# Storing most of an attention-and-MoE output as fp16 tiles cast by the software DMA queue instead of fp32 tiles on the sync queue

## The chip, the cores and the metric

The kernel runs on one core of a Trainium2 chip. The metric is the device time of one execution in microseconds (us). Times are medians of several executions. The span of a profiled execution, which the trace covers, is about 2 us shorter than the time. "Software queue" is the DMA queue that GpSimd (POOL) feeds, "sync queue" the one that SyncE (SP) feeds. The profile counts the packets of both queues against the same 16 DMA engines of the core.

## The reference

Sliding-window attention, plain in half of the heads and dilated in the other half, is followed by a soft mixture of experts. Only the last line of it matters here: each of 4608 rows is a weighted sum of 32 expert slots, and the result is 4608 x 512 in fp32, 9.44 MB.

```python
def _moe_ref(x, phi, w1, w2):
    logits = x @ phi                                    # 4608 x 32
    # ... slot inputs, one two-layer MLP for each of 8 experts -> slot_out (32 x 512)
    c = logits - logits.max(1, keepdims=True)
    c = np.exp(c)
    c /= c.sum(1, keepdims=True) + 1e-09
    return (c @ slot_out).astype(np.float32)            # 4608 x 512
```

## The kernel before

The attention and the experts' first layer take until about 140 us and aren't touched. While they run, GpSimd loads the experts' weights with a cast from fp32 to fp16. At the end these loads are what the kernel waits for. So `slot_out` is computed in two halves of 256 columns: the left half of `w2` of the last two experts is loaded first, and the left half of the output for the first 8 row pairs (a pair is 256 rows) is computed and stored while the right half of the weights still comes in. Then follow 10 pairs of whole rows, and last the right halves of the first 8 pairs.

```python
out_pool = tc.alloc_tile_pool(name="outp", bufs=NSPLIT // 2)          # 8 buffers for "ot"

def combine(half, pair):                                              # 256 rows x 256 columns
    # ... two matmuls into a PSUM tile fp [128, 2, 256]
    ot = out_pool.tile([128, 2, NH], FP32, name=f"ot{half}_{pair}", tag="ot")
    # even pair: two ScalarE activations; odd pair: one VectorE multiply; both: ot = fp * rrow
    nc.sync.dma_start(out=out[r0 : r0 + 256, NH * half : NH * half + NH]..., in_=ot)

def combine_full(pair):                                               # 256 rows x 512 columns
    ot = out_pool.tile([128, 2, DMODEL], FP32, name=f"of_{pair}", tag="of", bufs=5)
    # ... one matmul, and one eviction for each 128 rows: k = 0 on ScalarE, k = 1 on VectorE
    nc.sync.dma_start(out=out[r0 : r0 + 256, :]..., in_=ot)

# slot_out(half, experts): matmuls into PSUM; after the last expert ScalarE copies the half to so_sb
slot_out(0, ORDER[:6]); slot_out(1, ORDER[:6]); slot_out(0, HALVED)
for pair in range(8):                    # left halves; one expert of slot_out(1) after pair 5
    combine(0, pair)
    # ...
slot_out(1, HALVED[1:])
for pair in range(8, 18):
    combine_full(pair)
for pair in range(8):
    combine(1, pair)                     # right halves
```

The softmax here doesn't subtract the row's maximum and nothing guards it: scores larger than these inputs give would overflow.

## Time and profile before

| what | value | where it is read |
|---|---|---|
| time | 184.87 us (184.70 to 185.29, 4 runs) | times |
| span of the profiled run | 182.8 us | page |
| last weight load landed | 156.95 us | chain |
| stores under way | 155 to 181.3 us | windows, DMA packets |
| rate of whole-row stores (2 KB packets) | 384 GB/s | windows, 161 to 170 us |
| rate of half-row stores (1 KB packets) | 342 to 344 GB/s | windows, 175 to 180 us |
| eviction of 128x512 | ScalarE 0.69 us, VectorE 0.75 us | tile view |

First the page of the kernel before: the busy share of the DMA engines (tenths, in 40 slices of the span), the rate in each slice, and the two DMA queues with packets, MB and share of the 16 engines' span.

```profile
DMA  5999999999999999999999999999999999999996
GB/s 88 195 198 211 203 208 206 211 209 204 213 207 204 213 208 204 213 208 204 213 208 204 212 212 213 216 214 214 215 214 216 196 196 183 328 376 387 380 351 219
...
q0 software_dynamic: 24640, 31.10, 97.6%
q1 hardware_dynamic: 7360, 9.56, 14.9%
```

The DMA engines are full in all slices but the first and the last. The first 33 slices show about 210 GB/s because loads are counted by their fp16 side: the page has 62.18 MB read from HBM for 31.10 MB in q0, so fp32 comes out of HBM at twice that rate. The last slices are the fp32 stores of the sync queue (q1), counted in full.

Now the windows view of the kernel before: start and end, length, then busy us of PE, PEld, DVE, ACT and POOL with the count of instructions, the granted PE clock, the DMA busy share and GB/s. The DMA share is the summed time of the packets over 16 engines; above 1.0, packets on one engine overlap in time.

```profile
161.00:163.00 2.00, 1.18 (x5) 0.29 (x3) 0.80 (x2) 0.16 (x1) 0.00 (x0) 1.00 1.05 385
...
165.00:170.00 5.00, 3.07 (x11) 1.22 (x10) 3.27 (x5) 3.10 (x6) 0.00 (x0) 0.66 1.04 384
...
175.00:178.00 3.00, 0.00 (x0) 0.00 (x0) 0.00 (x0) 0.00 (x0) 0.00 (x0) 0.50 1.03 344
178.00:180.00 2.00, 0.00 (x0) 0.00 (x0) 0.00 (x0) 0.00 (x0) 0.00 (x0) 0.50 1.03 342
```

In these stretches, and in those left out between 159 and 180 us, the DMA share never falls under 1.0, while VectorE and ScalarE are each busy for two thirds of a stretch at most between 161 and 175 us, and idle after that. Nothing but the stores sets the pace here.

The chain of waits of the kernel before (start, length, what) tells the same.

```profile
146.53 10.42 DMA w<-in_moe_w_dram
...
157.33 0.38 ACT so_sb L689
...
158.17 3.00 ACT of L732 x5
...
162.03 10.45 DMA out_dram<-of x2
```

The last load lands at 156.95 us, ScalarE copies the right half of `so_sb`, evictions start, and then the stores fill the rest. Two lines of ScalarE's timeline (start, busy us, what, idle time before it and what ended it) show when that happens: the evictions of left pair 6, and the copy.

```profile
155.90 0.84 ACT L709 ACTIVATE ot<-f,rrow 128x256 f32<-128x256 f32 x2 [0.67 <-PE f L697]
157.33 0.37 ACT L689 CAST so_sb<-so 128x256 f16<-128x256 f32 x1 [0.59 <-PE so L681]
```

Line 792 is the end of the program; the columns are count, shortest/median/longest in ns, and first to last start in us.

```profile
L792 POOLq EVENT_SEMAPHORE  x4: 17/17/17, 182.1 to 182.7; - x4
L792 POOLq DRAIN  x3: 51/98/11675, 146.5 to 182.5; - x3
L792 SPq DRAIN  x3: 7/7/7, 182.0 to 182.3; - x3
```

SP starts its end routine (its first DRAIN) at 182.0 us, when all stores have landed. POOL's long DRAIN began at 146.5 us, together with GpSimd's last load issue, and took 11.7 us, so it was over at 158.2 us and nobody noticed. POOL's first semaphore of the final barrier comes at 182.1 us, right behind SP.

### The profile page before, as it was taken

How to read it: one execution, taken by the hardware profiler on the slowest of the kernel's cores; microseconds unless marked ns; L12 is line 12 of the kernel's file. 1: busy time of each engine (PE TensorE's matmuls, PEld its weight loads, DVE VectorE, ACT ScalarE, POOL GpSimd, SP SyncE). 2: the span in 40 equal slices, each digit the busy share in tenths (PEclk: the TensorE clock that was granted, in tenths of full speed). 3: DMA queues.
4: the chain of work that ended last, by engine and by line, in shares of the span. 5: the costliest groups of instructions: out<-in, count | busy, mean ns of one | idle time of the engine just before them, and what ended most of it. 6: DMA issues, size and time to landing. Idle time of an engine off the chain costs nothing.

```text
span 182.8 us, 5535 instructions
## 1 busy us (share of the span) xinstructions
PE 142.9 (78%) x2448; PEld 85.6 (47%) x2448; DVE 104.2 (57%) x225; ACT 90.1 (49%) x161; POOL 62.6 (34%) x86
## 2 busy tenths in 40 slices
PE   0467989999999999999999999998694087746600
PEld 0134556557557557557557557573532063312300
DVE  2585797958767867867867865360502004555700
ACT  2044267667666766766766766734002005644800
POOL 7643644652651751751822935311110110000000
PEclk9999999999999999999999999985569667897555
DMA  5999999999999999999999999999999999999996
GB/s 88 195 198 211 203 208 206 211 209 204 213 207 204 213 208 204 213 208 204 213 208 204 212 212 213 216 214 214 215 214 216 196 196 183 328 376 387 380 351 219
DMA packets 32024, 41.01 MB, mean 224 GB/s; under 512 B 2144, under 2 KB 19680, under 8 KB 32000
## 3 DMA queue, kind: packets, MB, share of 16 engines
q0 software_dynamic: 24640, 31.10, 97.6%
q1 hardware_dynamic: 7360, 9.56, 14.9%
q8 instruction: 19, 0.31, 0.6%
q14 instruction: 5, 0.04, 0.1%
HBM read 62.18 MB, written 9.44 MB: 392 GB/s over the span
## 4 chain that ended last, share of the span: by engine, by line
DMA 48%; PE 27%; issue 7%; ACT 6%; POOL 4%; DVE 3%; SPq 0%; POOLq 0%
DMA w<-in_moe_w_dram 34%; DMA raw<-in_q_dram 8%; DMA out_dram<-of 6%; PE lg L413 5%; PE o_p L344 5%; PE sa L287 4%; ACT p L298 4%; PE sa L276 3%; PE sb L276 3%; ACT of L732 2%; PE u L455 2%; PE rd L394 1%; PE vb L188 1%; PE va L188 1%; POOL w L220 1%
## 5 line engine op out<-in xcount | busy, mean ns | idle before, releaser
L298 ACT ACTIVATE p<-sa 128x960 f16<-128x960 f32 (+2 forms) x24 | 21.4, 890 | 30.2 <-PE sb L287 29.5
L344 PEld LDWEIGHTS <-p 128*128 128x128 f16 (+2 forms) x544 | 19.5, 98 | 12.6 <-issue 8.6
L241 DVE STREAM_TRANSPOSE qk<-raw 128x576 uint32<-128x576 uint32 x16 | 20.0, 1250 | 6.8 <-DMA raw<-in_q_dram 5.9
L250 DVE STREAM_TRANSPOSE qk<-raw 128x320 uint32<-128x320 uint32 (+1 forms) x32 | 21.5, 678 | 0.3
L298 ACT ACTIVATE p<-sb 128x960 f16<-128x960 f32 (+2 forms) x24 | 21.2, 885 | 0.0
L276 PE MATMUL sa<-masks,ident 128*128 128x480 f16 (+2 forms) x48 | 13.8, 372 | 6.6 <-DMA ident<-ident_d 4.9
L413 PE MATMUL lg<-xTd,phi 128*128 128x288 f16 x32 | 18.3, 659 | 0.0
L287 PE MATMUL sa<-qk 32*128 32x160 f16 (+4 forms) x416 | 15.7, 212 | 2.4 <-DVE qk L241 2.4
L287 PEld LDWEIGHTS <-qk 32*128 32x128 f16 x832 | 11.9, 96 | 11.8 <-issue 8.2
L276 PEld LDWEIGHTS <-ident 128*128 128x128 f16 x96 | 8.9, 102 | 17.4 <-issue 8.7
L216 POOL COPY v<-v 32x1024 f16<-32x1024 f16 x8 | 8.3, 1034 | 25.4 <-DVE v L209 22.9
L344 PE MATMUL o_p<-v,p 128*128 128x65 f16 (+1 forms) x288 | 16.4, 201 | 0.7 <-ACT v L197 0.7
L287 PE MATMUL sb<-qk 32*128 32x160 f16 (+4 forms) x416 | 15.7, 212 | 0.0
L232 POOL DMA_DIRECT2D w<-in_moe_w_dram x8 | 5.9, 742 | 27.2 <-DMA w<-in_moe_w_dram 22.8
L366 DVE TENSOR_TENSOR xp<-o_p,rc_p 128x448 f16<-128x448 f32 (+1 forms) x24 | 14.5, 602 | 0.8
L366 DVE TENSOR_TENSOR xd<-o_d,rc_d 128x448 f16<-128x448 f32 (+1 forms) x24 | 14.5, 602 | 0.8
L713 DVE TENSOR_TENSOR ot<-f,rrow 128x512 f32<-128x512 f32 x8 | 5.5, 690 | 15.8 <-PE f L697 15.6
L276 PE MATMUL sb<-masks,ident 128*128 128x480 f16 (+2 forms) x48 | 14.0, 372 | 0.4 <-issue 0.2
L681 PE MATMUL so<-w,hTm 128*32 128x256 f16 x128 | 7.0, 354 | 8.5 <-DMA w<-in_moe_w_dram 7.7
L220 POOL DMA_DIRECT2D w<-in_moe_w_dram x16 | 11.4, 715 | 5.5 <-DMA raw<-in_k_dram 2.1
L188 PE MATMUL va<-vs,orders 32*128 32x256 f16 (+1 forms) x96 | 12.1, 289 | 1.0 <-ACT p L298 1.0
L417 ACT ACTIVATE ET<-lg 128x288 f16<-128x288 f32 x16 | 6.6, 410 | 12.0 <-PE lg L413 11.8
(84 smaller groups left out, 251.7 us busy)
## 6 DMA issues: line engine op xcount, KB each, us to landing
w<-in_moe_w_dram POOLq DMA_DIRECT2D x16, 512.0 KB, 16.6
w<-in_moe_w_dram POOLq DMA_DIRECT2D x6, 1024.0 KB, 28.1
out_dram<-of SPq DMA_DIRECT2D x10, 512.0 KB, 5.5
vs<-in_v_dram POOLq DMA_DIRECT2D x8, 512.0 KB, 13.1
out_dram<-ot SPq DMA_DIRECT2D x16, 256.0 KB, 3.9
raw<-in_q_dram POOLq DMA_DIRECT2D x7, 576.0 KB, 15.1
raw<-in_k_dram POOLq DMA_DIRECT2D x7, 576.0 KB, 15.4
w<-in_moe_w_dram POOLq DMA_DIRECT2D x8, 256.0 KB, 23.3
```

Of the source, the lines that this page charges most:

```text
L188: nc.tensor.matmul(o.rearrange("p (h d) -> p h d", h=4), l, st[:, 0:4, D * r : D * r + D], start=(r == 0), stop=(r == DIL - 1), skip_group ...
L216: nc.gpsimd.tensor_copy(out=vL[b % NV][0:32, :, :, 0:D], in_=vD[b % NV][96:128, :, :, 0:D])
L220: nc.gpsimd.dma_start(out=w1t[e][:, 2 * i : 2 * i + 2, :], in_=src[:, 2 * i : 2 * i + 2, :])
L241: nc.vector.transpose(out=dst, in_=src)
L250: nc.vector.transpose(out=o, in_=i)
L276: nc.tensor.matmul(sps[h // 2][:, h % 2, 0:n], ident, bias[g], start=True, stop=False, skip_group_check=True,)
L287: nc.tensor.matmul(sps[h // 2][:, h % 2, c0 : c0 + w], kt_[32 * h : 32 * h + 32, k0 : k0 + 128, tt], qt_[32 * h : 32 * h + 32, q0 : q0 + w ...
L298: nc.scalar.activation(out=pt, in_=sps[ab][:, :, 0:n], func=AF.Exp, scale=SCALE)
L344: nc.tensor.matmul(o[p0 : p0 + np_, n, :], l, rr, start=(k == 0), stop=(k == len(jobs) - 1), skip_group_check=True,)
L366: nc.vector.tensor_tensor(out=x.rearrange("p t (h d) -> p (t h) d", h=4)[0:nq, u0:u1, :], in0=o[0:nq, 0:n, 0:D], in1=rc[0:nq, 0:n, None].b ...
L413: nc.tensor.matmul(lp, phi4[:, kc].rearrange("p c s -> p (c s)"), rhs, start=(kc == 0), stop=(kc == 3))
L681: nc.tensor.matmul(so[half][32 * a : 32 * a + 32, :], hTm[2 * g + c // 4][:, c % 4, 32 * j : 32 * j + 32], w2t[e][:, c, NH * half : NH * h ...
```

## The change

The intent: half of the bytes are read from SBUF for most stores, output tiles are half as big, so that there can be more of them, and the right halves don't wait for the end. A casting DMA has to be issued by GpSimd: the Trainium skill, "DMA: Bandwidth & Descriptors", section "SWDGE vs HWDGE vs iDMA", lists a cast during DMA as possible on the software queue only. The left halves stay on the sync queue in fp32, since they run beside the last loads.

```diff
-    out_pool = tc.alloc_tile_pool(name="outp", bufs=NSPLIT // 2)
+    out_pool = tc.alloc_tile_pool(name="outp", bufs=1)
 ...
     def combine(half, pair):
-        ot = out_pool.tile([128, 2, NH], FP32, name=f"ot{half}_{pair}", tag="ot")
+        ot = out_pool.tile([128, 2, NH], (FP32, FP16)[half], name=f"ot{half}_{pair}", tag=f"ot{half}", bufs=6 + 2 * half)
 ...
-        nc.sync.dma_start(
+        (nc.sync, nc.gpsimd)[half].dma_start(
 ...
     def combine_full(pair):
-        ot = out_pool.tile([128, 2, DMODEL], FP32, name=f"of_{pair}", tag="of", bufs=5)
+        ot = out_pool.tile([128, 2, DMODEL], FP16, name=f"of_{pair}", tag="of", bufs=7)
 ...
-        nc.sync.dma_start(
+        nc.gpsimd.dma_start(
 ...
         for pair in range(NSPLIT // 2, NFIN // 2):
             combine_full(pair)
-        for pair in range(NSPLIT // 2):
-            combine(1, pair)
+            if pair >= NFIN // 2 - NSPLIT // 2:
+                combine(1, pair - (NFIN // 2 - NSPLIT // 2))
```

## The prediction

> **What bounds the kernel now.** The chain of waits ends with weight loads (the last lands at 156.95 us), one PE and ACT step each, five ACT evictions, and then 10.45 us of stores. From 155 us on the windows show the DMA engines at a busy share of 1.03 to 1.05 until 181 us, while PE, ACT and DVE are half idle. So the last 25 us are DMA time: 9.44 MB of output. While 2 KB packets (whole rows) are stored the windows show 383 to 386 GB/s, while 1 KB packets (halves) are stored 343 to 357.
>
> **What the change does not remove.** HBM still gets 9.44 MB of fp32. PE, ACT and DVE do the same instructions in another order. Evictions from PSUM (ACT 128x512 0.69 us, DVE 0.75 us) should keep their times. The Trainium skill, "DMA: Bandwidth & Descriptors", section "Issuing engines are not separate DMA queues", says that DMAs of all issuers share the same 16 engines and only issue time is saved. SP's issue time (0.66 us per half, 1.22 us per 512 KB) is hidden under the stores (1.37 us per 512 KB at 384 GB/s) already.
>
> **What it may gain.** The SBUF side of 18 stores (7.34 MB) is read as fp16. If the write side limits a store, nothing is gained. The casting loads of this trace run at 2 x 213 = 426 GB/s on their fp32 side (2 KB fp16 packets) and at 2 x 198 = 396 with 512 B fp16 packets. If casting stores reached those rates, whole rows would take 12.3 us in place of 13.7, right halves 5.3 in place of 6.0: at most 2 us. I expect about a third of it. More buffers (7 for 5) buy nothing where DMA is the limit.
>
> **What it costs.** Left halves have 6 buffers, not 8. Pair 6 on ACT now waits for pair 0's store. That was issued at 153.74 and takes 4.0 us to land, so ACT gets on at about 157.6 in place of 155.9. The second so_sb copy stands behind it on ACT and moves from 157.33 to about 158.5, the first whole row with it. Its store is issued at about 160.3 instead of 159.2, now by GpSimd (0.7 us issue, by the loads' issues). Left stores kept the engines busy until about 161, so some 0.5 to 1 us of DMA idleness appears between 159 and 162. The first left eviction and store lose their waits on eight load semaphores: 0.2 us gained.
>
> **Sum.** Delay +0.8, casting stores -0.7, start -0.2: 184.8 us, within 2%. Range 182.0 to 187.3. Faster by over 2%: 0.12. Within 2%: 0.78. Slower by over 2%: 0.10.
>
> **What would show the steps right.** (1) The span from 162 us to the end is full of DMA, with 384 to 400 GB/s of fp32 written (or half of it, if packets are counted by their fp16 side, as for the loads). (2) ACT waits for an output DMA before the pair-6 eviction, and so_sb's second copy starts 1 to 1.5 us later. (3) GpSimd issues take 0.6 to 0.9 us and aren't in the chain. (4) ACT and DVE end several us earlier, and the end is still a store landing.
>
> **What would make it wrong.** The cast may have its own rate: above 420 GB/s written gives 183 or less; 330 gives 187. If the engines' cost follows the fp16 side, stores could nearly halve and the kernel gains 5 us or more. The software queue may start later or fall behind. The left stores' landing, which shares the engines with the last loads, may be later than 4 us and stretch the gap.

## The result, and the profile after

The changed kernel takes 186.02 us (185.76 to 186.38, 4 runs) against 184.87 us: ratio 1.006, 95% interval 1.0036 to 1.0085. That is 1.1 us slower, small but clear of noise. Ratios in this document are the mean time of one kernel's runs over the mean of the other's runs of the same rounds, so they aren't quite the ratios of the medians quoted. The result is correct in fp16, too.

The rates and queues of the page after:

```profile
GB/s 88 199 204 212 202 206 208 210 207 206 214 209 203 212 210 203 213 206 206 213 207 208 209 211 216 214 215 214 214 214 212 197 196 191 319 325 405 408 410 91
...
q0 software_dynamic: 29536, 38.44, 112.6%
q1 hardware_dynamic: 2464, 2.22, 3.7%
```

38.44 MB now go through the software queue (q0) and 2.22 MB through the sync queue. The last slices reach 405 to 410 GB/s, where before they had 376 to 387 and then 351; and the last slice has only 91. The windows after show both, and a hole:

```profile
161.00:163.00 2.00, 1.99 (x8) 0.93 (x7) 1.59 (x3) 1.67 (x5) 1.42 (x2) 0.65 0.61 198
163.00:165.00 2.00, 1.55 (x6) 0.57 (x6) 1.96 (x4) 1.90 (x5) 1.96 (x3) 1.00 1.48 420
165.00:170.00 5.00, 3.91 (x18) 1.62 (x17) 4.56 (x7) 4.69 (x10) 5.00 (x8) 1.00 1.60 408
...
175.00:178.00 3.00, 0.00 (x0) 0.00 (x0) 0.00 (x0) 0.00 (x0) 0.03 (x1) 0.50 1.58 410
178.00:180.00 2.00, 0.00 (x0) 0.00 (x0) 0.00 (x0) 0.00 (x0) 0.00 (x0) 0.50 1.64 406
```

Two differences stand out against the same windows before. From 163 us on the stores run at 406 to 420 GB/s instead of 342 to 384. Between 161 and 163 us the DMA share falls to 0.61 (before: 1.05); a finer cut has 0.13 from 161.6 to 162.6 us, so the engines are idle for about one microsecond. ScalarE's timeline shows where that comes from:

```profile
157.84 0.84 ACT L709 ACTIVATE ot<-f,rrow 128x256 f32<-128x256 f32 x2 [2.09 <-DMA out_dram<-ot]
158.57 0.37 ACT L689 CAST so_sb<-so 128x256 f16<-128x256 f32 x1
```

ScalarE waited 2.09 us for an output DMA before the eviction of left pair 6 (its buffer is that of pair 0, which had to land first), and the copy of `so_sb` stands behind it in order: it starts at 158.57 instead of 157.33 us. VectorE waits likewise for pair 7. The first whole-row store is issued at 161.36 us instead of 159.20.

The end of the chain view after, and line 792 after:

```profile
173.83 0.47 issue
174.30 0.73 POOLq L792
```

```profile
L792 POOLq EVENT_SEMAPHORE  x4: 17/17/17, 183.4 to 184.0; - x4
L792 POOLq DRAIN  x3: 51/98/9061, 174.3 to 183.9; - x3
L792 SPq DRAIN  x3: 7/7/7, 181.8 to 183.6; - x3
```

The chain view is no help with the end: it is followed back from the last instruction that isn't the sequencer's, here GpSimd's last store issue, and stops at 175.03 us (before: at 173.15, with an eviction). Line 792 is where to look. SP's first DRAIN is at 181.8 us, so the stores were all in a little earlier than before (182.0). But POOL's long DRAIN, begun at 174.30 us, took 9.06 us and ended at 183.36 us. POOL's first semaphore of the final barrier comes at 183.4 us, 1.6 us behind SP. The span ends at 184.1 us. That wait is new.

The trace records when each store landed. With that, the difference of the two spans can be taken apart without a remainder (us):

| stretch | before | after | difference |
|---|---|---|---|
| up to the last left half's landing | 162.44 | 162.89 | +0.45 |
| from there to the last landing | 19.22 | 18.50 | -0.72 |
| from the last landing to the end of the span | 1.16 | 2.76 | +1.60 |
| span | 182.82 | 184.15 | +1.33 |

The first row is within the scatter of the runs: in the thirteen profiles the first left store is issued between 153.06 and 154.35 us, by kernels that hardly differ up to there. The second row holds a gain and the hole of 1 us. The third row is the drain.

### The profile page after: what moved, and what is told of

Same layout as the page of the kernel before. It is cut to its first block, busy times and chain, and to the rows that moved or that the text cites. A ratio compares the mean times of both kernels' runs of the same rounds, so it can differ in the third digit from the quotient of the medians. Undisturbed runs are those within 1.5% of the kernel's fastest.

```text
span 184.1 us, 5522 instructions
## 1 busy us (share of the span) xinstructions
PE 142.3 (77%) x2448; PEld 85.5 (46%) x2448; DVE 104.8 (57%) x225; ACT 90.0 (49%) x161; POOL 75.1 (41%) x104
## 3 DMA queue, kind: packets, MB, share of 16 engines
q0 software_dynamic: 29536, 38.44, 112.6%
q1 hardware_dynamic: 2464, 2.22, 3.7%
## 4 chain that ended last, share of the span: by engine, by line
DMA 42%; PE 30%; ACT 8%; issue 6%; POOL 6%; DVE 3%; POOLq 0%; DVEq 0%; ACTq 0%
DMA w<-in_moe_w_dram 27%; DMA vs<-in_v_dram 7%; DMA raw<-in_q_dram 6%; PE lg L413 5%; PE o_p L344 4%; PE sa L287 4%; ACT p L298 4%; PE sa L276 3%; PE sb L276 3%; ACT ot L709 3%; DMA out_dram<-ot 2%; PE f L730 2%; PE u L455 1%; PE rd L394 1%; PE vb L188 1%
## 5 line engine op out<-in xcount | busy, mean ns | idle before, releaser
L713 DVE TENSOR_TENSOR ot<-f,rrow 128x512 f32<-128x512 f32 (+1 forms) x8 | 5.5, 688 | 18.6 <-PE f L697 15.5
L743 POOL DMA_DIRECT2D out_dram<-of x10 | 7.0, 701 | 15.1 <-ACT of L732 14.0
```

## The experiments

Theory: three effects add up. (1) The cast makes the stores faster. (2) Six left buffers delay the whole rows and leave a DMA hole. (3) GpSimd's end-of-program drain outlasts the last landing of the software queue, which costs nothing as long as the sync queue ends last, and 1.6 us where the software queue ends last. Rivals: for (1), the software queue as such or the new order; for (2), GpSimd's later issue; for (3), a long backlog of the software queue, or its being used for outputs at all. Eleven kernels ran, all with correct results; the kernel before had medians of 184.73, 184.60 and 184.59 us.

### Eight left buffers in the changed kernel

```diff
-tag=f"ot{half}", bufs=6 + 2 * half)
+tag=f"ot{half}", bufs=8 - half)
```

(The space allows 8 + 7, not 8 + 8.)

> The changed kernel with 8 left buffers (and 7 right ones) instead of 6 (and 8). Theory (six left buffers stall ACT at pair 6 and open two DMA gaps, 0.4 us at 158 and 1.1 us at 162): the wait of ACT for an output DMA before pair 6 is gone, the second so_sb copy is back at 157.3 to 157.7, the DMA share stays at 0.9 or more from 157 to 162 us except for at most 0.5 us, and the span is 1.0 to 1.5 us shorter than the changed kernel's 184.1: 182.6 to 183.1. Rival (the gap comes from GpSimd's late first issue and the software queue's start, not from the buffers): the gap at 162 stays, the span gains less than 0.5 us.

Measured: 185.17 us, ratio 1.0028 (1.0015 to 1.0041). ScalarE's timeline has the copy back in its old place, and the windows have no hole:

```profile
157.24 0.37 ACT L689 CAST so_sb<-so 128x256 f16<-128x256 f32 x1 [0.61 <-PE so L681]
```

```profile
161.00:163.00 2.00, 1.45 (x8) 0.67 (x7) 1.96 (x4) 1.89 (x5) 2.00 (x4) 1.00 1.36 394
...
165.00:170.00 5.00, 2.04 (x10) 0.76 (x8) 3.21 (x5) 2.41 (x5) 4.37 (x7) 0.98 1.67 409
...
178.00:180.00 2.00, 0.00 (x0) 0.00 (x0) 0.00 (x0) 0.00 (x0) 0.00 (x0) 0.50 1.07 244
```

The hole at 161 to 163 us is gone (share 1.36). From 165 to 170 us the stores still run at 409 GB/s, and by 180 us the data are done: the last landing is at 180.31 us, against 181.66 before. Still the span is 183.2 us, longer than before. Line 792 of this run shows why:

```profile
L792 POOLq EVENT_SEMAPHORE  x4: 17/17/17, 182.3 to 183.1; - x4
L792 SPq DRAIN  x3: 7/7/7, 180.7 to 182.5; - x3
```

SP is ready at 180.7 us, POOL at 182.3. The buffers cost 0.3% (1.006 less 1.0028), 0.6 us, but the two ratios come from different calls and their intervals overlap slightly, so the size is rough; I had expected 1.0 to 1.5 from the profile, which gave 0.97. The rival for (2) falls: GpSimd's issue at 159.61 us came early enough to leave no hole.

### The software queue without the cast

```diff
 # the kernel before
-        nc.sync.dma_start(                      # in combine
+        (nc.sync, nc.gpsimd)[half].dma_start(
-        nc.sync.dma_start(                      # in combine_full
+        nc.gpsimd.dma_start(
```

> The kernel before, with whole rows and right halves issued by GpSimd on the software queue but still fp32 (no cast), order and buffers as before. Theory A (the faster stores of the changed kernel, 408 GB/s against 384 and 348, come from the halved SBUF read of the cast): rates stay at 380 to 386 GB/s for whole rows and 343 to 357 for halves, DMA share near 1.0, span 184 to 185 (end delayed by the GpSimd drain). Theory B (the software queue itself keeps more packets under way): 404 GB/s or more with a DMA share of 1.4 or more in both, span 182.5 to 183.5. Either way, theory of the end (GpSimd's last drain outlasts the last software landing by about 1.6 us): 3.0 us or more from the last DMA bytes to the end of the span, against 1.7 before.

Measured: 187.85 us, ratio 1.0174 (1.0154 to 1.0193). Its windows:

```profile
161.00:163.00 2.00, 0.52 (x2) 0.10 (x1) 0.14 (x1) 0.00 (x0) 1.62 (x3) 1.00 1.02 370
...
165.00:170.00 5.00, 2.95 (x10) 1.24 (x10) 3.09 (x5) 2.90 (x6) 2.68 (x4) 0.60 1.01 370
...
175.00:178.00 3.00, 0.00 (x0) 0.00 (x0) 0.00 (x0) 0.00 (x0) 1.64 (x3) 0.71 1.01 326
```

Whole rows at 370 GB/s, halves at 326, with a share of 1.0: not faster but slower than from the sync queue (384 and 344). So the software queue as such isn't the reason for the gain; it comes with the cast. One caution: the form of the packets changes with it. From 165 to 170 us this kernel's software queue moved 1.85 MB in 512 packets (4 KB each, apart from some of 4 bytes), one after the other (share 1.01); the changed kernel's moved 2.04 MB in 1331 (2 KB and 1 KB by the fp32 side), and they overlap (share 1.60). A casting packet of 2 KB takes longer than a plain one of the sync queue, 114 ns against 88 in the mean; the higher rate goes with the overlap. Whether fewer bytes read from SBUF or the form of the packets brings it, no run separates. The absence of a bandwidth gain fits the Trainium skill, "DMA: Bandwidth & Descriptors", section "Issuing engines are not separate DMA queues", by which another issuer saves only the time to issue; here some bandwidth was even lost. The span ends 2.76 us after the last landing, as in the changed kernel, with fp32 tiles: the drain has nothing to do with the cast. Neither theory had the lower rates, and the span, 185.6 us, lies above both ranges.

### The order alone

```diff
 # the kernel before
             combine_full(pair)
-        for pair in range(NSPLIT // 2):
-            combine(1, pair)
+            if pair >= NFIN // 2 - NSPLIT // 2:
+                combine(1, pair - (NFIN // 2 - NSPLIT // 2))
```

> The kernel before, with only the order changed: right halves between whole rows, still fp32 on the sync queue. Theory (the order by itself brings nothing, the cast brings the rate): same time as before, ratio 0.997 to 1.003, last sync landing 1.1 to 1.3 us before the end of the span, DMA at 360 to 385 GB/s with a share near 1.0. Rival (mixing 1 KB and 2 KB packets is what made the stores of the changed kernel faster): 395 GB/s or more from 164 us on and a span of 182 or less.

Measured: 184.48 us, ratio 0.9988 (0.9972 to 1.0004). Its windows have 366 to 369 GB/s from 165 to 178 us, which lies between the 384 of whole rows and the 344 of halves. So the order by itself does nothing to the time that shows.

### Six left buffers alone

```diff
 # the kernel before
-    out_pool = tc.alloc_tile_pool(name="outp", bufs=NSPLIT // 2)
+    out_pool = tc.alloc_tile_pool(name="outp", bufs=6)
```

> The kernel before, with only 6 buffers for the half-width tiles instead of 8. Theory (six left buffers hold ACT at pair 6 until pair 0 has landed, and that delays the second so_sb copy and the first whole row): ACT idles 1.5 to 2.2 us for an output DMA before pair 6, the second so_sb copy starts at 158.2 to 158.8, the first whole-row store is issued at 160.2 to 160.8, a DMA dip of 0.3 to 1 us follows near 161, and the time is 0.3 to 1.0 us over the kernel before. Rival (the dip needs the software queue's late start): ACT waits, but the time is within 0.3 us of before.

Measured: 185.53 us, ratio 1.0044 (1.0029 to 1.0059), so 0.8 us. ScalarE's timeline and the window of the hole:

```profile
158.73 0.84 ACT L709 ACTIVATE ot<-f,rrow 128x256 f32<-128x256 f32 x2 [2.87 <-DMA out_dram<-ot]
159.46 0.37 ACT L689 CAST so_sb<-so 128x256 f16<-128x256 f32 x1
```

```profile
161.00:163.00 2.00, 2.00 (x7) 0.73 (x6) 1.79 (x3) 1.63 (x4) 0.00 (x0) 0.59 0.74 260
```

The wait, 2.87 us, and with it the delay of the copy (159.46 us) were larger in this profile than I had said, since pair 0 landed only at 158.63 us (the profiled execution, 186.40 us, was the slowest of the seven); the time is within the range. The same mechanism therefore works with the sync queue alone: (2) is the buffers' doing. One caution: the right halves have 6 buffers here, too, and some of their evictions waited as well, though the sync queue was issuing without a pause by then.

### Whole rows by the software queue, right halves by the sync queue

```diff
 # the kernel before
-        ot = out_pool.tile([128, 2, DMODEL], FP32, name=f"of_{pair}", tag="of", bufs=5)
+        ot = out_pool.tile([128, 2, DMODEL], FP16, name=f"of_{pair}", tag="of", bufs=10)
-        nc.sync.dma_start(                      # in combine_full
+        nc.gpsimd.dma_start(
```

> The kernel before, with only the whole rows as fp16 on the software queue (10 buffers); left and right halves in fp32 on the sync queue, right halves last as before. Theory (drain hidden when the sync queue ends last; whole rows faster by the cast): the software queue ends 2 us or more before the sync queue, the GpSimd drain ends before the last sync landing, 1.7 us or less from the last bytes to the end, whole rows alone at 405 to 416 GB/s, span 181.0 to 182.2, faster than the kernel before by 0.5 to 1.8 us. Rival (the tail belongs to the kernel's end whenever GpSimd issued any output): 3 us or more from last bytes to the end, span not below 183.

Measured: 184.18 us, ratio 0.9973 (0.9960 to 0.9987): faster than before by 0.3%.

```profile
L792 POOLq DRAIN  x3: 51/98/13548, 165.9 to 182.4; - x3
L792 SPq DRAIN  x3: 7/7/7, 181.8 to 182.2; - x3
```

The software queue's last store landed at 177.84 us, POOL's drain was over at 179.49 us, the sync queue's last landed at 181.40 us, and the span ended 1.28 us later. So the drain is hidden, and the rival that any output from GpSimd costs a tail falls. The span, 182.7 us, missed the expected range: whole rows did run at 413 GB/s, but while both queues were active, the rate was 373 to 384.

### Right halves by the software queue, whole rows by the sync queue

```diff
 # the kernel before
-        ot = out_pool.tile([128, 2, NH], FP32, name=f"ot{half}_{pair}", tag="ot")
+        ot = out_pool.tile([128, 2, NH], (FP32, FP16)[half], name=f"ot{half}_{pair}", tag="ot")
-        nc.sync.dma_start(                      # in combine
+        (nc.sync, nc.gpsimd)[half].dma_start(
```

> The kernel before, with only the right halves as fp16 on the software queue, the whole rows in fp32 on the sync queue. Whole rows run at 384 GB/s until the right halves join at about 170 us; then both queues share. If the software queue ends last or within 1 us of the sync queue, the theory of the end wants the span to end 1.4 to 1.7 us after the last software landing: span 182.5 to 184. If mixed queues run at the faster rate, the last bytes are moved 0.5 to 1.0 us earlier than before.

Measured: 185.85 us, ratio 1.006 (1.0044 to 1.0076). The last landing (181.31 us, on the software queue) is 0.35 us earlier than before, with halves at 395 GB/s instead of 344; POOL's drain ended 1.56 us after it, and the span 2.35 us after it (I had expected 1.4 to 1.7 for the span, which fits the drain alone). The kernel is 1.7 us slower than the one above, where the queues are exchanged; 1.07 us of it is the longer end (2.35 against 1.28), with the software queue last. The rest isn't taken apart: the two kernels also differ in how many bytes are cast and in buffers.

### The last pairs of whole rows by the sync queue

Both kernels are the changed kernel with 8 left buffers. All fp16 stores come first; then the last four pairs, or the last one, are evicted as fp32 blocks of 128 rows and stored by the sync queue.

```diff
 # the changed kernel; LAST = 4, and LAST = 1
-        for pair in range(NSPLIT // 2, NFIN // 2):
-            combine_full(pair)
-            # ... right halves between them
+        first, stop = NSPLIT // 2, NFIN // 2 - LAST
+        for pair in range(first, stop):
+            combine_full(pair)                       # fp16, software queue
+            if pair >= first + 2:
+                combine(1, pair - first - 2)         # fp16, software queue
+        for pair in range(stop - first - 2, NSPLIT // 2):
+            combine(1, pair)
+        for pair in range(stop, NFIN // 2):
+            combine_rows(pair)                       # two [128, 512] fp32 tiles, sync queue
```

> Candidate for the best: the changed kernel with 8 left buffers, and the last four pairs of whole rows (2.1 MB) in fp32 on the sync queue, after all fp16 stores. Theory of the end: the software queue's last landing is 2 us or more before the sync queue's, the GpSimd drain ends (1.6 to 2.0 us after the last software landing) before the sync queue is done, and the span ends 1.1 to 1.3 us after the last sync landing. With 408 GB/s for the casting part: span 180.9 to 181.9, time 182.8 to 183.7, ratio 0.989 to 0.995. Rival (mixing the two queues costs as much as the cast gains): ratio 0.996 to 1.000.

> The same, with only the last pair of whole rows (0.5 MB) in fp32 on the sync queue. Theory of the end: 0.5 MB is not enough to outlast the software queue by 1.6 us, so the drain is still exposed: the span ends 2.6 to 2.9 us after the last software landing, span 182.3 to 183.3, slower than the kernel with four pairs by 0.7 to 1.8 us. Rival (it is the last output's queue that decides, whatever lies in the other one): span as with four pairs.

Measured: with four pairs 186.07 us (ratio 1.0074, 1.0061 to 1.0087), with one 185.22 us (ratio 1.0034, 1.0016 to 1.0051). I had the first one wrong, and the order of the two as well. With four pairs the software queue did not end first: its last landing was at 181.79 us, the sync queue's at 181.62. The two queues of that run between 175 and 177 us (packets, MB, share) show how that came about:

```profile
q1 hardware_dynamic: 262, 0.49, 90.4%
q0 software_dynamic: 264, 0.26, 47.9%
```

They got the same number of packets, 262 and 264, but those of the sync queue are 2 KB and those of the software queue, right halves by then, 1 KB. The Trainium skill, "DMA: Bandwidth & Descriptors", section "Queues, rings and completion order", says that each engine goes round-robin between queues by whole packets, each of which typically holds several descriptors. Equal counts agree with taking turns; whether a "packet" of this profile is one of the page's, no run shows. So the software queue fell behind and ended last, and the span ended 2.6 us after its last landing, as the theory of the end has it for that case. With one pair, the sync queue was done at 178.05 us and the software queue at 181.32; the span ended 2.7 us later, as expected, though at 184.0 us it lies above the expected range. Neither hides the drain; so they don't contradict the theory, but the plan for the first one was bad.

### One late store on the software queue, and its control

In the kernel before, the last store (256 KB) is made to come late: its buffer is that of right half 3, so it can be evicted only when that one has landed. The first kernel stores it as fp16 by GpSimd, the control as fp32 by SP.

```diff
 # the kernel before; the control has sw = False
+        sw = half == 1 and pair == 7
+        late = half == 1 and pair in (3, 7)
-        ot = out_pool.tile([128, 2, NH], FP32, name=f"ot{half}_{pair}", tag="ot")
+        ot = out_pool.tile([128, 2, NH], FP16 if sw else FP32, name=f"ot{half}_{pair}",
+                           tag="late" if late else "ot", bufs=1 if late else 7)
-        nc.sync.dma_start(                      # in combine
+        (nc.gpsimd if sw else nc.sync).dma_start(
```

> The kernel before, with the single last store (right half of pair 7, 256 KB of 9.44 MB) as fp16 on the software queue; its buffer is the one of right half 3, so that its eviction, and so its issue, comes after that one's landing and it lands last. Theory of the end (GpSimd's final drain lasts 1.6 to 2.0 us past the last software landing, and the span ends 0.7 to 0.8 us after it): the span ends 2.6 to 2.9 us after the last landing, and the kernel is slower than its control with the same store in fp32 on the sync queue by 1.2 to 1.8 us. Rival (the tail comes from the long backlog of the software queue): one short store leaves a tail of 1.1 to 1.6 us and the two kernels are within 0.4 us of each other.

> The control: the same buffers and the same late last eviction, but that store in fp32 on the sync queue. Both theories: the span ends 1.1 to 1.3 us after the last landing, and GpSimd's drain ends at 158 to 159 us. Time 0 to 1 us above the kernel before for the delayed last store.

Measured: 186.55 us (ratio 1.0096, 1.0075 to 1.0118) against the control's 185.13 us (ratio 1.0012, 0.9984 to 1.0040), 1.4 us for the queue of one store that holds 1/36 of the bytes. The end of the program with the software store, then that of the control:

```profile
L797 POOLq EVENT_SEMAPHORE  x4: 17/17/17, 183.7 to 184.3; - x4
L797 POOLq DRAIN  x3: 51/98/3853, 179.8 to 184.2; - x3
L797 SPq DRAIN  x3: 7/7/7, 182.7 to 183.9; - x3
```

```profile
L797 POOLq EVENT_SEMAPHORE  x4: 17/17/17, 182.7 to 183.3; - x4
L797 POOLq DRAIN  x3: 51/97/11667, 146.7 to 183.2; - x3
L797 SPq DRAIN  x3: 7/7/7, 182.6 to 182.9; - x3
```

In the first, POOL's drain began at 179.8 us and took 3.85 us. It ended at 183.65 us, 1.28 us after the store's landing at 182.37; SP had been ready at 182.7. The span ended 2.06 us after the landing, less than the 2.6 to 2.9 that I had expected. In the control the drain ended at 158 us, SP and POOL are ready together, and the span ends 1.16 us after the last landing. So 0.9 us of the 1.4 come from the end. The store's own path is longer, too: from the landing of right half 3 to that of the last store it was 3.93 us by GpSimd and 3.06 us by SP. The two shares add up to more than 1.4, as each comes from one profile. The rival "only a long backlog makes a tail" falls. So does the milder form, that a backlog makes it longer. The time from the software queue's last landing to the end of POOL's drain, in all thirteen traces by the number of stores that GpSimd issues (each kernel has the same 66 loads besides):

| software stores | 0 | 1 | 8 | 10 | 14 | 16 | 17 | 18 |
|---|---|---|---|---|---|---|---|---|
| drain ends after the last landing, us | 1.24 | 1.28 | 1.56 | 1.64 | 1.81 | 1.89 | 1.93 | 1.97 |

That is 1.24 us and 0.041 us more for each store. DMAs still under way when the drain begins don't set it: there are 8 in the kernel before, which has the shortest tail, and 6 to 8 in all others but this one. Nor do bytes, packets or the cast: all three kernels with 18 stores, the one without a cast among them, have 1.97. Fewer and larger software stores should then shorten it a little; no run tried that.

### A version that beats both

The lesson of the experiments put together: 8 left buffers; fp16 and the software queue for all right halves and eight pairs of whole rows; the last two pairs in fp32 by the sync queue, held back until the software queue is nearly done, so that the queues don't mix for long. The hold is a buffer: these tiles take the buffers of whole pair 14 and right half 6.

```diff
 # the changed kernel; combine_rows as above, its first two tiles with tags "g1" and "g2", bufs=1
+        tag, bufs = (("ot0", 8), ("g2", 1) if pair == 6 else ("ot1", 5))[half]    # in combine
+        tag, bufs = ("g1", 1) if pair == 14 else ("of", 6)                        # in combine_full
+        after_row = {10: (0,), 11: (1,), 12: (2,), 13: (3, 4, 5), 14: (6,), 15: (7,)}
+        for pair in range(NSPLIT // 2, 16):
+            combine_full(pair)
+            for p in after_row.get(pair, ()):
+                combine(1, p)
+        combine_rows(16)
+        combine_rows(17)
```

> Candidate for the best: 8 left buffers; eight whole pairs and all right halves as fp16 on the software queue; the last two whole pairs (1.05 MB) in fp32 on the sync queue, held back until whole pair 14 and right half 6 have landed (they use those buffers), so that the queues mix little and the sync queue ends last. Theory: 405 GB/s or more up to about 176 us, the sync queue's last landing 2 us or more after the software queue's last, the drain hidden, the span ends 1.1 to 1.3 us after the last landing: span 181.2 to 182.2, ratio 0.991 to 0.997. If the gate opens too late, a DMA gap shows before the sync stores; if too early, the software queue ends within 1.9 us of the sync queue and the span ends 2.6 us or more after its last landing: ratio 0.998 to 1.003.

Measured: 183.65 us, ratio 0.9947 (0.9925 to 0.9970): 0.9 us under the kernel before and about 2 us under the changed one (1.1% by the ratios). It was run at another time. Its windows and its end:

```profile
170.00:175.00 5.00, 0.00 (x0) 0.00 (x0) 0.00 (x0) 0.00 (x0) 1.64 (x3) 0.64 1.73 405
175.00:178.00 3.00, 0.00 (x0) 0.00 (x0) 1.41 (x2) 1.27 (x2) 0.00 (x0) 0.50 1.36 376
```

```profile
L812 POOLq EVENT_SEMAPHORE  x4: 17/17/17, 181.0 to 181.7; - x4
L812 POOLq DRAIN  x3: 51/98/8513, 171.2 to 181.5; - x3
L812 SPq DRAIN  x3: 7/7/7, 181.0 to 181.3; - x3
```

The casting stores run at 405 GB/s until 175 us, and the hole at 161 us isn't there (share 1.32 from 161 to 163 us). POOL's drain ends at 179.67 us (171.16 plus 8.51), 1.9 us after the software queue's last landing at 177.78; the sync queue's last landing is at 180.75 us, SP and POOL are ready together at 181.0, and the span ends at 181.8. From 175 to 178 us, where the software queue runs out and the sync queue sets in, the rate is 376 GB/s.

## Why the prediction was right or wrong

The total, 184.8 us with a range of 182.0 to 187.3, held 186.02; "within 2%" was right. That says little for the sum that led to it: it was 1.2 us too low and had no change where the kernel became 1.1 us slower. It lacked a term of 1.6 us, and part of that was made up by luck, as the faster stores gave 0.55 us more than it had. The range was wide enough for the missing term even without that.

- **What bounds the kernel.** Right: the stores' DMA time from 155 us on. What moved the time in the experiments was the stores' rate, a hole in the stores, or what follows the last one.
- **"Delay +0.8".** Right in mechanism, and in size within what two rough measures tell. ScalarE got on at 157.84 us (predicted 157.6), the copy moved to 158.57 (158.5). GpSimd's first issue came at 161.36, a microsecond later than the 160.3 predicted: VectorE had waited for its buffer as well, and GpSimd began the issue 0.57 us after the second eviction's end, SP before only 0.06 us. The hole was about 1 us (0.5 to 1). Undoing it gained 0.6 us; doing it alone cost 0.8 us.
- **"Casting stores -0.7".** Right in direction, too small. I allowed "at most 2 us" and took a third. From the last left landing to the last landing it is 19.22 us before and 17.96 us with 8 left buffers: -1.26 us. The windows from 165 us on show 406 to 410 GB/s, above the 384 to 400 of step (1) and within the 396 to 426 that the loads had suggested.
- **"Start -0.2".** Not seen. The first left store came 0.39 us later, not earlier, in the profile after; the thirteen profiles scatter by 1.3 us there, so 0.2 us couldn't show.
- **The missing term.** The sum had no term for the end of the program: step (4) said that "the end is still a store landing". It isn't: it is GpSimd's drain, and from the last landing to the end of the span it is 2.76 us instead of 1.16, +1.60 us. The profile before had the sign of it: POOL's drain ended at 158.18 us, 1.24 us after the last load. I had not looked at it, and it was off the critical path until the change made GpSimd the last to issue. Step (3) had the issue times right (0.70 to 0.72 us) and looked no further than the issues: GpSimd held up the end by its drain.
- **The sum as measured.** +0.6 for the buffers, -1.26 for the faster stores, +1.6 for the drain: about +0.9 us (an estimate that mixes times and one profile's intervals), against 1.1 us measured.

What stays open: why a casting store is faster. Half as many bytes are read from SBUF, and that is what the change set out to use, but no run tells that apart from some other property of a casting DMA, such as its packets, which overlap. And what POOL's drain does after the last landing, and why each software store adds 0.041 us to it, no trace shows.

## What to carry to other kernels

Before the last stores are moved to another queue, look at the end of the program, too: which engine's drain is then the last, and is it hidden behind another queue's stores? A casting store is worth trying where stores bound the kernel, but let the sync queue have the last stores (here 1.05 MB), held back until the software queue is nearly empty. And count buffers along each engine's order: an eviction that waits for a buffer also holds up whatever stands behind it on the same engine, here a copy on which everything else depended.

## What the Trainium skill lacked or had wrong

- "DMA: Bandwidth & Descriptors" has no rate for stores that cast. Here fp16 to fp32 stores ran at 405 to 410 GB/s, counted by their fp32 side, against 384 (2 KB packets) and 344 (1 KB) for plain stores from the sync queue.
- The same page's section "Issuing engines are not separate DMA queues" speaks of no cost of another issuer, and where the page calls the sync and scalar queues generally faster ("Issuing engine by pattern") it gives no store rates. Here the same fp32 stores were slower from GpSimd: 370 against 384 GB/s for whole rows, 326 against 344 for halves, and the kernel 1.7% slower, 1.6 us of it at the end.
- No page that I read tells that GpSimd's drain at the end of the program outlasts its last DMA. "VectorE: DVE Perf Modes", section "The DRAIN you can't avoid", speaks of drains of the preamble and postamble of about 12 ns on all five engines. At the end of this program SP's took 7 ns, but POOL's ended 1.24 to 1.97 us after the last landing of the software queue, 0.041 us later for each store that GpSimd had issued. Whether these are the drains that the page means, no run shows.
- "DMA: Bandwidth & Descriptors", section "Queues, rings and completion order", says that an engine takes turns between the queues that have work. Once both were served, packets were indeed shared one to one (262 and 264). But a queue that joined while the other had a backlog started late: 3.3 to 4.5 us from the first issue to the first packet in four runs, the joining queue being the sync queue in three and the software queue in one, against 0.84 us in the kernel that held its sync stores back, and 1.3 to 1.9 us where the software queue joined while the last left halves were still on their way. The page has nothing on that.
